# Fewer scores ahead at the start, tiles turned inside the first layers, and the last pair's lists made later, in an attention and mixture-of-experts kernel

## The chip, the cores and the metric

The kernel runs on one core of one Trainium2 chip. The metric is the device time of one execution in microseconds (us), as the median of several runs. Profiles come from one execution taken by the hardware profiler. The engines are TensorE (PE, with its weight loads shown apart as PEld), VectorE (DVE), ScalarE (ACT), GpSimd (POOL) and SyncE (SP, which here only issues transfers). Each engine works through its own instructions in the order in which the program gave them.

## What is computed

Attention with a sliding window of 128 and a linear position bias runs over 8 batches, 8 heads, 576 positions and a head size of 64. Its output, 4608 rows of 512, goes through a mixture of 8 experts: a gate picks one expert for each row, each expert is two layers with a ReLU between, and the row is scaled with the gate's probability.

```python
scores = scale * np.matmul(q, k.transpose(0, 1, 3, 2))
scores = np.where(mask, scores + bias[None], -1000000000.0)
attn = np.exp(scores - max); attn = attn / (sum + 1e-09)
x = (attn @ v).transpose(0, 2, 1, 3).reshape(4608, 512)
expert_idx = np.argmax(x @ w_gate, axis=1)
...
    h = np.maximum(x_sorted[lo:hi] @ w1[e], 0.0)
    y_sorted[lo:hi] = h @ w2[e]
return gate_w[:, None] * y
```

## The kernel before

**Order.** The program fixes the order of the instructions on each engine by the order of its own statements; nothing is rearranged afterwards. Small jobs are put into lists (`tasks` during attention, `fill` during the experts), and one entry is taken off at set points: `some()` once in each attention group, `step()` after each half product of an expert's layer.

**Attention.** Batches are taken two at a time (four pairs, `bp`), heads two at a time, which gives 16 units of four groups each, 64 groups in all. For each group `scores(i)` multiplies keys and queries into a PSUM tile `sp` (two buffers), ACT takes the exponential into `pe` (six buffers), and DVE multiplies by position factors. `values(u, half, kbs)` then multiplies with the values, and `finish(u, half)` copies the half unit out and sums the weights. The loop issues `scores(i + AHEAD)` before the values of group i, with `AHEAD = 3`. Loads for unit u + 2 are issued in unit u on SP's queue, each held back by `no_earlier_than`, a tiny transfer that waits for the product of group i + 1.

**Routing.** What `behind(bp)` lists runs during the next pair's attention: the gate, the choice of an expert, each row's place in its expert's list (`place`), and the lists themselves. `ones_at` and `ones_at2` (L1000 to L1015) make tables of ones on DVE and `enlist` (L1025) turns them into lists with matmuls. `early_table` computes the gather index of the first expert and `gather` fetches its rows from `x_rows` in DRAM with four indirect transfers on POOL. Rows reach `x_rows` by `row_out` (POOL) and `squares_out` (POOL or SP). The last pair has no attention behind which its routing could run; `with_tail` puts it into the first layer of the first expert.

**Experts.** A first group of 512 rows for each expert is `fixed[e]`; overflow of 128 rows goes to small groups between them. Both layers use seven products instead of eight for a 2 by 2 block matrix (`strassen1`, `strassen2`), each product in two halves, so 14 steps a layer, in the order of products 1, 2, 6, 5, 7, 3, 4. `prepare(g)` makes the jobs that come before: `to_scale` (DVE, L1252) and `to_columns` (PE transposes, L1265, then an ACT copy) for each of four tiles, `x_sums` (four DVE sums, of which product 6 reads the second) and `w1_sums` (eight). Products 1 and 2 read tiles 0 and 1 only. The sums of w2 and of h (L530 to L541) are needed from product 6 of the second layer. `count_all`, `check_all`, `table_further` and `pieces` compute the overflow's index. `end_of_tail` frees the routing buffers and loads the second expert's weights into that space.

Of the kernel before, what the change touches and what calls it, by code (L numbers as in the profile page):

```python
# [8 lines left out]
F32 = mybir.dt.float32  # L9
# [7 lines left out]
P = 128  # L17
# [441 lines left out]
def kernel(  # L459
# [12 lines left out]
    nc = tc.nc  # L472
# [12 lines left out]
    TPB = 2 * S // P  # L485
# [21 lines left out]
    with ExitStack() as fast:  # L507
# [504 lines left out]
        def ones_at2(bp):  # L1012
            rc, oc = slot_of[bp], oc_of[bp]
            orow = small.tile([P, TPB, P], BF16, name="gsr")
            nc.vector.tensor_tensor(  # L1015
                orow[:], K["cols"][:, None, :].to_broadcast([P, TPB, P]),
                rc[:, 0, :].unsqueeze(2).to_broadcast([P, TPB, P]), op=ALU.is_equal,
            )
            oh_of[bp] = oc, orow

        def enlist(bp):
            oc, orow = oh_of[bp]
            ps = ps_m.tile([P, 512], F32, name="m")
# [44 lines left out]
        def scales_squared(bp):  # L1068
# [10 lines left out]
            for r in range(2):  # L1079
                half = slice(r * KB, (r + 1) * KB)  # L1080
                nc.scalar.copy(sq[half].rearrange("p t k h -> p k t h"), ps5[half, :, :, r, :])  # L1081

        def squares_turned(bp, t):
            if bp in spare and t < TPB - 1:
                w = NA * PW
                flat = spare[bp].rearrange("p h n -> p (h n)")
                xs = flat[:, t * w : (t + 1) * w].rearrange("p (k w) -> p k w", k=NA)
            else:
                xs = rows.tile([P, NA, PW], F32, name="xs")
            xs_of[bp, t] = xs  # L1090
            nc.vector.transpose(
                xs[:, :, :PD].rearrange("p k (h j) -> p k h j", h=HP),
                xT[bp][:, :, t * P : (t + 1) * P].rearrange("p h (k i) -> p k h i", k=NA),
            )

        def squares_out(bp, t, eng, n=1):

            for k in range(t, t + n):
                nc.gpsimd.tensor_copy(xs_of[bp, k][:, :, PD:], sq_of[bp][:, k])  # L1099
            if n == 1:  # L1100
# [50 lines left out]

        def early_table():

# [4 lines left out]
            nc.vector.tensor_scalar_max(hole[:], hole[:], 0.0)  # L1158
            nc.vector.tensor_tensor(K["off"][:, 0:1], K["off"][:, 0:1], hole[:], op=ALU.add)
            tok = rte.tile([P, NJ], F32, name="tok_0")  # L1160
            number(tok[:], lambda k: parts[:, k, 0, :NJ])
# [92 lines left out]
        def to_columns(g, j):  # L1254
# [12 lines left out]
            else:  # L1267
                nc.vector.transpose(to.rearrange("p h (k j) -> p k h j", j=TQ), xn[:])  # L1268

        def x_sums(g):  # L1270
            x = g["xT"]
            g["xs"] = mx_pool.tile([P, 3, 2, 256], F32, name="xs")
            o = g["xs"]
            return sums_t(
                x[:, 0:2, :256], x[:, 0:2, 256:], x[:, 2:4, :256], x[:, 2:4, 256:], o[:, 0], o[:, 1], o[:, 2],
            )
# [11 lines left out]
        def prepare(g):  # L1288
# [8 lines left out]
            if n == NJ:  # L1297
                sums = later(lambda: x_sums(g), 4)
                if "ws" not in g:
                    sums += later(lambda: w1_sums(g), 8)  # L1300
                if g is fixed[1]:
                    todo[-1].append(sums.pop(0))
                    todo += [sums[k : k + 2] for k in range(0, len(sums), 2)]
                else:
                    todo += [[f] for f in sums]
            return [(g, t) for t in todo]


        def behind(bp):
# [10 lines left out]
            if bp == 0:  # L1320
                rt = [lambda t=t: squares_turned(bp, t) for t in range(TPB)]
                ro = [lambda t=t: squares_out(bp, t, nc.gpsimd) for t in range(TPB)]
                return [g3[0:1], g3[1:2], g3[2:] + t3[0:1], t3[1:], a, a2 + rt[0:1], b + rt[1:2], b2 + rt[2:3],
                        c + n + rt[3:4], [], q + p, p2 + ro[0:4], o, o2, rt[4:6], e + rt[6:8] + ro[4:8]]
            rt, ro = ([lambda t=t, f=f: f(bp, t) for t in range(TPB)] for f in (row_turned, row_out))
            if bp == 1:
                last = [lambda: squares_turned(0, TPB - 1), lambda: squares_out(0, TPB - 1, nc.gpsimd)]
                return [g3[0:1] + last, g3[1:2], g3[2:] + t3[0:1], t3[1:], a + rt[0:1], a2 + rt[1:2], b + rt[2:3],
                        b2 + rt[3:4], c + n, [], p + ro[0:2], p2 + ro[2:4] + rs[4:5], o + rs[5:6], o2 + rs[6:7], rs[7:8], e + rs[8:9]]
            return [g3, t3, a + a2, b + b2 + rt[0:1], c + n + rt[1:2], rt[2:4], p + p2 + ro[0:4], o + o2 + rs[4:6], rs[6:9],  # L1330
                    e, [early_table, lambda: gather(fixed[0], x_d[: 3 * 2 * S, :])]]

# [7 lines left out]
        NG = 4 * len(units)  # L1340
        AHEAD = 3
        for i in range(AHEAD):
            scores(i)
        route_consts()
# [4 lines left out]
        for i in range(NG):  # L1349
# [13 lines left out]
            if g == 2:  # L1363
                values(u, 0, (4,))
                finish(u, 0)
                some()
            if i + AHEAD < NG:
                scores(i + AHEAD)
            if u in (10, 11):
# [9 lines left out]
            else:  # L1379
                values(u, 1, (6, 7, 8))  # L1380
                finish(u, 1)
            if u == len(units) - 1 and g == 0:
                tasks.extend(t for _, t in prepare(fixed[0]))
            if g != 2:
# [29 lines left out]

        def strassen1(g, start=None):
            w, x, ws, xs = g["w1"], g["xT"], g["ws"], g["xs"]
            hf = F // 2
# [186 lines left out]

        self_late = []

        def with_tail(g, w2s):
# [3 lines left out]
            rt = [lambda t=t: squares_turned(bp, t) for t in range(TPB)]  # L1611
            ro = [lambda: squares_out(bp, 0, nc.sync, 4), lambda: squares_out(bp, 4, nc.sync, 4), lambda: squares_out(bp, 8, nc.sync)]
            w = [[f] for f in w2s]
            a, b, p, o = (
                [lambda f=f, f2=f2: (f(bp), f2(bp))]
                for f, f2 in ((scale_a, scale_a2), (scale_b, scale_b2), (place, place2), (ones_at, ones_at2))
            )
            c, n, q, e = ([lambda f=f: f(bp)] for f in (scale_c, count, scales_squared, enlist))
            todo = [
                [lambda k=k: gate(bp, k) for k in range(3)] + rt[0:1], [lambda k=k: turn(bp, k) for k in range(3)] + rt[1:2],  # L1620
                a, rt[2:3], b, rt[3:4], c + n, rt[4:5] + w[0], q + p + ro[0:1] + rt[8:9], rt[5:6] + o, rt[6:8] + ro[2:3],
                ro[1:2] + w[1] + w[2], e + w[3], [table_fixed] + w[4] + w[5],
            ]
            self_late.extend(w[6] + w[7])
            return [(g, t) for t in todo]
# [5 lines left out]
        for i in range(len(groups)):  # L1631
# [3 lines left out]
            if i == 0:  # L1635
                strassen1(g, start=with_tail)
                end_of_tail()
                fill.append((g, [lambda: gather(fixed[1], x_d[:, :]), self_late[0]]))
                fill.append((g, [self_late[1], count_all]))
                fill.append((g, [check_all]))  # L1640
                fill.append((g, [table_further]))
                fill.append((g, [next_groups, lambda: pieces(slice(NJ, E * NJ), "1")]))
                fill.append((g, [lambda: pieces(slice(E * NJ, NC), "2")]))
                fill.extend(prepare(fixed[1]))
                strassen2(g)
                w_of = lambda k: (w1_a, w2_a) if k % 2 == 0 else (lp["w"], lp["w"])
                load_w1(groups[2], w1_a)
# [52 lines left out]
```

## Time and profile before

| | |
|---|---|
| median of 3 runs | 686.86 us (684.91 to 687.83) |
| the profiled execution | 691.06 us, its span 689.2 us |
| mean granted TensorE clock | 0.985 |
| DMA moved | 122.00 MB, mean 177 GB/s |
| POOL gathers, L1240 | 124, 1008 ns each |
| largest single wait of PE at the start | 4.3 us, for the first queries and keys |
| PE waits in 165 to 182 us | 3.1 us, two, for DVE's scaled tiles L1252 |
| PE waits in 211 to 245 us | 2.2 and 1.4 us, for DVE |

The span goes from the first to the last instruction. PE is busy nearly always, so a job on another engine matters only where PE stands waiting for it. In the rows of the timeline the square bracket names the idle time before an instruction and what ended it. Attention lasts to about 181 us, the first expert's first layer to 211, its second to 245, and the second expert's first layer to 269 us.

### The profile page before, as it was taken

What the parts mean: (1) busy time and instruction counts of PE and PEld (TensorE: products, weight loads), DVE (VectorE), ACT (ScalarE), POOL (GpSimd) and SP (SyncE); (2) the same over time, 40 slices, a digit from 0 to 9 for tenths busy, and PEclk for the clock granted to TensorE, in tenths of its full rate; (3) what the DMA queues carried; (4) which work ended last, traced back from release to release, by engine and by line L of the source; (5) the groups of instructions that cost most, each with busy time, mean ns of one, the idle gap of its engine ahead of it and who ended that gap; (6) DMA issues with size and microseconds to landing.
All of it is one profiled execution on the core that took longest, in us unless ns stands there. A gap on an engine that the chain in (4) does not pass through costs nothing.

```text
span 689.2 us, 14460 instructions
## 1 busy us (share of the span) xinstructions
PE 655.8 (95%) x6004; PEld 548.2 (80%) x6004; DVE 379.4 (55%) x717; ACT 199.2 (29%) x365; POOL 237.6 (34%) x360
## 2 busy tenths in 40 slices
PE   5899889998999899999999999999999999999996
PEld 4778768687687788878897887888788978878893
DVE  4567769786489476614842564275148435633500
ACT  5555446465331223113202310231131123002210
POOL 8100572215001176117323702652172247023020
PEclk9999899999999999999999999999999999999999
DMA  9677987854516964185448237652844573284010
GB/s 285 200 222 192 287 241 219 289 157 149 165 22 162 386 206 140 57 292 170 155 154 301 57 129 258 212 166 63 296 137 145 178 276 97 86 305 154 1 62 8
DMA packets 63549, 122.00 MB, mean 177 GB/s; under 512 B 5905, under 2 KB 30001, under 8 KB 63474
## 3 DMA queue, kind: packets, MB, share of 16 engines
q1 hardware_dynamic: 51778, 92.78, 42.0%
q0 software_dynamic: 10544, 27.31, 12.4%
q8 instruction: 49, 0.80, 0.5%
q10 hardware_dynamic: 1152, 0.88, 0.4%
q14 instruction: 26, 0.21, 0.1%
HBM read 101.79 MB, written 19.96 MB: 177 GB/s over the span
## 4 chain that ended last, share of the span: by engine, by line
PE 75%; issue 9%; DVE 8%; DMA 4%; POOL 2%; ACT 1%; SPq 0%; POOLq 0%; DVEq 0%; ACTq 0%
PE sp L769 5%; PE at L804 5%; PE pair0b L1511 4%; PE pair0a L1511 4%; PE pair0b L1454 4%; PE pair0a L1454 4%; PE pair1a L1511 4%; PE pair1b L1511 4%; PE pair2b L1454 4%; PE pair1b L1454 4%; PE pair1a L1454 4%; PE pair2a L1454 4%; PE pair2a L1511 4%; PE pair2b L1511 4%; PE m L836 3%
## 5 line engine op out<-in xcount | busy, mean ns | idle before, releaser
L1240 POOL DMA_INDIRECT xg<-x_rows,p_idx x124 | 125.0, 1008 | 37.8 <-issue 37.5
L1534 POOL DMA_INDIRECT out_dram<-zo,s_idx x39 | 44.5, 1140 | 250.6 <-DVE zo L1525 149.6
L769 PE MATMUL sp<-q_sb,k_sb 64*64 64x192 f32 (+2 forms) x1152 | 60.2, 331 | 7.1 <-DMA q_sb<-in_qT_dram 6.9
L775 ACT ACTIVATE pe<-sp 128x768 f32<-128x768 f32 x64 | 51.9, 811 | 49.6 <-PE sp L769 46.7
L804 PE MATMUL at<-pe,v_sb 64*64 64x192 f32 (+2 forms) x1408 | 59.6, 289 | 3.4 <-issue 3.4
L778 DVE TENSOR_TENSOR pe<-pe,fac 128x768 f32<-128x768 f32 x48 | 45.5, 952 | 28.3 <-ACT pe L775 27.8
L804 PEld LDWEIGHTS at<-pe,v_sb 64*64 64x64 f32 x1408 | 48.0, 138 | 9.5 <-issue 6.9
L769 PEld LDWEIGHTS sp<-q_sb,k_sb 64*64 64x64 f32 x1152 | 42.0, 141 | 16.6 <-DMA q_sb<-in_qT_dram 4.3
L1465 ACT ACTIVATE h<-h 128x512 f32<-128x512 f32 x32 | 20.2, 631 | 41.3 <-DVE h L1464 41.3
L836 PE MATMUL m<-pe,ind 128*32 128x192 f32 (+2 forms) x704 | 29.8, 288 | 0.6 <-issue 0.6
L1252 DVE TENSOR_TENSOR xn<-xg 128x512 f32<-128x512 f32 x39 | 26.3, 676 | 3.4 <-DMA xg<-x_rows,g_idx 3.1
L836 PEld LDWEIGHTS m<-pe,ind 128*32 128x32 f32 x704 | 23.2, 110 | 3.0 <-issue 1.0
L1108 POOL DMA_DIRECT2D x_rows<-xs x40 | 21.6, 548 | 6.4 <-POOL xs L1099 1.9
L783 DVE TENSOR_TENSOR pe<-pe,fac 128x768 f32<-128x768 f32 x16 | 15.3, 955 | 15.2 <-ACT pe L775 15.1
L1268 DVE STREAM_TRANSPOSE xgT<-xn 128x512 f32<-128x512 f32 x31 | 22.1, 712 | 1.1
L538 DVE TENSOR_TENSOR w2s<-w 128x512 f32<-128x512 f32 x16 | 10.9, 684 | 19.4 <-DMA w<-in_moe_w_dram 19.4
L1099 POOL COPY xs<-sq 128x16 f32<-128x16 f32 x10 | 2.6, 258 | 53.8 <-ACT sq L1081 53.8
L1566 PE MATMUL pair2a<-w,h 128*128 128x512 f32 x48 | 21.1, 592 | 0.0
L821 ACT COPY xT<-at 128x640 f32<-128x640 f32 (+1 forms) x32 | 18.7, 585 | 6.5 <-PE at L804 4.6
L1454 PE MATMUL pair0b<-xgT,w 128*128 128x256 f32 x72 | 17.2, 382 | 0.0
L1511 PE MATMUL pair1a<-w,h 128*128 128x256 f32 x72 | 17.0, 379 | 0.0
L1454 PE MATMUL pair0a<-xgT,w 128*128 128x256 f32 x72 | 17.0, 379 | 0.0
(375 smaller groups left out, 1393.2 us busy)
## 6 DMA issues: line engine op xcount, KB each, us to landing
w<-in_moe_w_dram SPq DMA_DIRECT2D x29, 2048.0 KB, 7.9
k_sb<-in_kT_dram SPq DMA_DIRECT2D x15, 576.0 KB, 5.6
q_sb<-in_qT_dram SPq DMA_DIRECT2D x15, 576.0 KB, 5.6
v_sb<-in_v_dram SPq DMA_DIRECT2D x30, 288.0 KB, 4.5
x_rows<-xs POOLq DMA_DIRECT2D x16, 264.0 KB, 3.8
x_rows<-xs POOLq DMA_DIRECT2D x32, 66.0 KB, 4.7
x_rows<-xT SPq DMA_DIRECT2D x8, 264.0 KB, 5.2
w<-in_moe_w_dram SPq DMA_DIRECT2D x4, 512.0 KB, 7.7
```

What stands on the lines that cost most here:

```text
L769: nc.tensor.matmul(sp[c * KB : (c + 1) * KB, r, c0 : c0 + n], lhsT=k_sb[u][hs, c, kb * KB : (kb + 1) * KB], rhs=q_sb[u][hs, c, kb * KB : k ...
L775: nc.scalar.activation(pe[:], sp[:, :, :GC], AF.Exp, scale=SCALE)
L778: nc.vector.tensor_tensor(pe.rearrange("p r (k c) -> p r k c", k=2), pe.rearrange("p r (k c) -> p r k c", k=2), fac[:, h0 : h0 + 2, None, ...
L804: nc.tensor.matmul(acc[r * D : (r + 1) * D, c, lo - q0 : hi - q0], lhsT=v_sb[u][c * KB : (c + 1) * KB, kb, r * D : (r + 1) * D], rhs=pe[c ...
L836: nc.tensor.matmul(sm[32 * j : 32 * j + 32, lo - q0 : hi - q0], lhsT=none[:] if pe is None else ind[:, hp, :], rhs=fac[:, 0, :KB] if pe is ...
L1108: eng.dma_start(x_d[r0 : r0 + n * m, a * PW : (a + 1) * PW].rearrange("(k i) w -> i k w", i=TQ), xs[a * TQ : (a + 1) * TQ, p0 // TQ : p0 / ...
L1240: nc.gpsimd.indirect_dma_start(out=to, out_offset=None, in_=where, in_offset=bass.IndirectOffsetOnAxis(ap=idx, axis=0),)
L1252: nc.vector.tensor_tensor(xn[:], x, s.unsqueeze(3).to_broadcast([P, NA, HP, TQ]), op=ALU.mult)
L1268: nc.vector.transpose(to.rearrange("p h (k j) -> p k h j", j=TQ), xn[:])
L1454: nc.tensor.matmul(ps[:, f * 256 : (f + 1) * 256], lhsT=left[m][:, d, fb * P : (fb + 1) * P], rhs=right[m][:, d, :], start=(m in (1, 2, 5) ...
L1511: nc.tensor.matmul(ps[:, :256], lhsT=left[m][:, f, c * P : (c + 1) * P], rhs=right[m][:, f, :], start=(m in (1, 2, 5) and f == 0), stop=Tr ...
L1534: ins = nc.gpsimd.indirect_dma_start(out=out[:, :], out_offset=bass.IndirectOffsetOnAxis(ap=s_idx[:, g["c0"] + j : g["c0"] + j + 1], axis= ...
```

## The change

The lead of the scores is two groups in units 0 and 1 and three from unit 2 on. The loop that copies the scales into the rows becomes a function of its own, `squares_scaled`, so that all nine tiles of the last pair are given their scales at once. The first part of `early_table` becomes `early_holes`; it and the rest run one step earlier, and with them the first gather.

For the first expert, `tasks` now gets only the first three entries of `prepare(fixed[0])` (scale of tile 0; columns of 0 and scale of 1; columns of 1 and scale of 2), after group 61 instead of 60. Columns of tiles 2 and 3, the last scale and the sums of x are put into steps 0 and 1 of its first layer. `with_tail` places the rest of the last pair's routing in other steps, all of the w2 sums in the first layer, and one row write on POOL instead of SP. `ones_at`, `ones_at2` and `enlist` of the last pair go to steps 0, 1 and 5 of the second layer, and `end_of_tail` to step 5; the table and gather of the second expert follow in step 6, then the counts and further tables. Tiles 0 and 1 of the second expert are turned in steps 11 and 12, and tiles 2 and 3 in steps 0 and 1 of its own first layer, with four of its weight sums; its x sums come in steps 2 and 3.

```diff
-        AHEAD = 3
-        for i in range(AHEAD):
-            scores(i)
+        scored = [0]
+
+        def scores_to(n):
+            while scored[0] < min(n, NG):
+                scores(scored[0])
+                scored[0] += 1
+
+        scores_to(2)
...
-            if i + AHEAD < NG:
-                scores(i + AHEAD)
+            scores_to(i + (3 if u < 2 else 4))
...
-            return [g3, t3, a + a2, b + b2 + rt[0:1], c + n + rt[1:2], rt[2:4], p + p2 + ro[0:4], o + o2 + rs[4:6], rs[6:9],
-                    e, [early_table, lambda: gather(fixed[0], x_d[: 3 * 2 * S, :])]]
+            return [g3, t3, a + a2, b + b2 + rt[0:1], c + n + rt[1:2], rt[2:4], p + p2 + ro[0:4], o + o2 + rs[4:6],
+                    rs[6:9] + [early_holes], e + [early_table, lambda: gather(fixed[0], x_d[: 3 * 2 * S, :])]]
...
+        def squares_scaled(bp, t, n=1):
+
+            for k in range(t, t + n):
+                nc.gpsimd.tensor_copy(squares(bp, k)[:, :, PD:], sq_of[bp][:, k])
+
         def squares_out(bp, t, eng, n=1):
-
-            for k in range(t, t + n):
-                nc.gpsimd.tensor_copy(xs_of[bp, k][:, :, PD:], sq_of[bp][:, k])
...
-            if u == len(units) - 1 and g == 0:
-                tasks.extend(t for _, t in prepare(fixed[0]))
+            if u == len(units) - 1 and g == 1:
+                first = [t for _, t in prepare(fixed[0])]
+                tasks.extend(first[:3])
...
-            ro = [lambda: squares_out(bp, 0, nc.sync, 4), lambda: squares_out(bp, 4, nc.sync, 4), lambda: squares_out(bp, 8, nc.sync)]
+            ro = [lambda: squares_out(bp, 0, nc.sync, 4), lambda: squares_out(bp, 4, nc.sync, 4), lambda: squares_out(bp, 8, nc.gpsimd)]
...
             todo = [
-                [lambda k=k: gate(bp, k) for k in range(3)] + rt[0:1], [lambda k=k: turn(bp, k) for k in range(3)] + rt[1:2],
-                a, rt[2:3], b, rt[3:4], c + n, rt[4:5] + w[0], q + p + ro[0:1] + rt[8:9], rt[5:6] + o, rt[6:8] + ro[2:3],
-                ro[1:2] + w[1] + w[2], e + w[3], [table_fixed] + w[4] + w[5],
+                first[3] + [lambda k=k: gate(bp, k) for k in range(3)],
+                first[4] + [lambda k=k: turn(bp, k) for k in range(3)] + first[5] + first[6] + first[7] + first[8],
+                a, a2 + rt[0:1], b, b2 + rt[1:2], c + n + rt[2:3], rt[3:4] + w[0] + w[1],
+                q + p + [lambda: squares_scaled(bp, 0, TPB)], rt[4:5] + rt[8:9] + ro[0:1] + ro[2:3] + w[2],
+                rt[5:8] + ro[1:2], w[3], w[4] + w[5], w[6] + w[7],
             ]
-            self_late.extend(w[6] + w[7])
+            after_tail.extend([o[0:1], o[1:2], [], [], [], e + [end_of_tail]])
...
-                end_of_tail()
-                fill.append((g, [lambda: gather(fixed[1], x_d[:, :]), self_late[0]]))
-                fill.append((g, [self_late[1], count_all]))
-                fill.append((g, [check_all]))
-                fill.append((g, [table_further]))
-                fill.append((g, [next_groups, lambda: pieces(slice(NJ, E * NJ), "1")]))
-                fill.append((g, [lambda: pieces(slice(E * NJ, NC), "2")]))
-                fill.extend(prepare(fixed[1]))
+                todo = [t for _, t in prepare(fixed[1])]
+                sums = [f for (f,) in todo[9:]]
+                now = after_tail + [
+                    [table_fixed, lambda: gather(fixed[1], x_d[:, :])], [count_all], [check_all], [table_further],
+                    [next_groups] + todo[0], todo[1], todo[2] + [lambda: pieces(slice(NJ, E * NJ), "1")],
+                    [lambda: pieces(slice(E * NJ, NC), "2")] + sums[0:4],
+                ]
+                fill.extend((g, t) for t in now)
                 strassen2(g)
+                fill.extend((None, t) for t in [todo[3] + sums[4:], todo[4], todo[5] + todo[6], todo[7] + todo[8]])
```

## The prediction

> **What bounds the kernel now.** I read the page's busy shares and 40 slices first, then the waits of TensorE (PE) by stretch, then PE's and VectorE's (DVE's) timelines inside the stretches that lose time, and last the chain of waits.
>
> ```profile
> PE 655.8 (95%) x6004; PEld 548.2 (80%) x6004; DVE 379.4 (55%) x717; ACT 199.2 (29%) x365; POOL 237.6 (34%) x360
> ...
> PEclk9999899999999999999999999999999999999999
> ```
>
> PE is busy for 655.8 of 689.2 us, so 33 us of gaps is all that an edit of order can win at full clock. Instructions on PE stay (the added and removed ones below are moves), so the question is which gaps close and which open. The table of stretches shows where they lie:
>
> ```profile
> 13.00:30.00 17.00, 14.92 (x396) 12.97 (x399) 7.54 (x9) 9.54 (x17) 6.28 (x51) 1.00 0.76 223
> 164.00:181.00 17.00, 13.86 (x296) 11.66 (x288) 8.65 (x23) 6.30 (x13) 5.15 (x6) 0.90 0.39 97
> 181.00:211.00 30.00, 29.36 (x167) 24.09 (x166) 23.93 (x61) 8.87 (x18) 1.33 (x9) 1.00 0.35 104
> 211.00:245.00 34.00, 30.46 (x150) 26.21 (x149) 23.55 (x65) 6.55 (x14) 7.54 (x7) 0.95 0.83 274
> 245.00:269.30 24.30, 24.30 (x114) 21.11 (x113) 15.75 (x26) 8.16 (x14) 18.40 (x20) 1.00 0.44 141
> ```
>
> (columns: stretch, length, busy us of PE, weight loads, DVE, ACT, POOL, then granted clock.) The first layer of the first expert (181 to 211) and everything from 245 to the last layer run without a gap. The edit can reach gaps in three places: the first units, the entry to the first expert, and its second layer (two waits):
>
> ```profile
> 13.04 0.88 PE L769 MATMUL sp<-q_sb,k_sb 64*64 64x192 f32 x16 [1.89 <-DMA q_sb<-in_qT_dram]
> ...
> 172.72 0.66 PE L1265 MATMUL m<-ident,xn 128*128 128x128 f32 x4 [2.48 <-DVE xn L1252]
> ...
> 220.68 1.13 PE L1511 MATMUL pair1a<-w2s,hs 128*128 128x256 f32 x4 [1.35 <-DVE w2s L539]
> ...
> 226.61 1.03 PE L1142 MATMUL m<-ta,to_squares 128*128 128x7 f32 x8 [2.19 <-DVE tb L1131]
> 227.50 2.72 PE L1511 MATMUL pair0a<-w2s,hs 128*128 128x256 f32 x8
> 230.01 2.88 PE L1511 MATMUL pair0b<-w2s,hs 128*128 128x256 f32 x8
> ```
>
> The last two rows are as telling as the waits: the same eight matmuls take 1.73 us start to start elsewhere, so after the 2.19 us gap PE ran below full clock until 232.7. The stretch 164 to 181 shows it too (granted 0.90): 48 small matmuls at 175.95 took 2.22 us where 24 take 0.84.
>
> **What the Trainium skill says.** "TensorE: Matmul & The Clock Gate", Part 1, says that the array falls to half clock once an activity window of about 3.4 us has seen too little work and needs about as long to return. The trace agrees in kind: gaps of 2.48 and 2.19 us were each followed by slow matmuls, the gap of 1.35 us at 219.3 by none. The same page ("Architectural detail") says matmuls stay in program order and DVE is a strict FIFO; here PE stood 2.48 us behind one transpose with other work queued. "DMA: Bandwidth & Descriptors", section on the anatomy of a DMA from GpSimd, puts a fixed cost of about 2 us on such a write before its completion shows; the row writes here land 2.5 to 3.3 us after issue.
>
> **The change, part by part.** All sums are against the profiled execution (691.06 us, span 689.2). It is 4.2 us above the median of the three runs (686.86); I take the gain in us over to the median.
>
> *A. Scores two groups ahead in the first two units.* Before, PE does scores of group 4 (first of unit 1) before the values of group 1, and there waits 1.89 us for unit 1's queries, whose transfer was issued at 4.71 and took 8.19 us by the chain of waits. After, the values of groups 1 and 2 and the first sums (from 13.71 to 15.40 in the timeline, 1.69 us) come before those scores, so the wait is filled and 0.2 us of it is left. At group 8 two scores are issued at once and the lead is three again. Nothing is added. The price: between a group's scores and its values PE now has two other groups, 4 x 0.83 = 3.3 us. The path it must cover, from the row at 16.77: matmuls end at 17.60, exp 17.66 to 18.47, multiply to 19.47, so 1.9 us, or 2.8 with one 0.93 us factor activation ahead on ACT. Unit 2's loads are paced by a product one group later (about 2 us); they landed 6 us after issue and are read at group 8, some 10 us on. The gain lies between 0.3 (stalls of 0.2 us in a few groups) and 1.9. I take 1.5.
>
> *B. Entry to the first expert.* Before, PE's order is: values, tile 0's transposes (wait 2.48), sums, tile 1, values, sums, tiles 2 and 3 (wait 0.65), first layer at 180.66. From 170.23, when it ran dry, that is 10.43 us for 5.5 us of work (16 transposes 1.7, 56 value matmuls 2.0, two sums 1.75); the rest is waiting and slow clock. The list step and the gather are put one step earlier, but I give that nothing: the gather at 167.98 waits for the row writes of the third pair, the last issued at 164.02 and landing up to 3.3 us later, and those stay where they are; the index was ready at 166.0. So tile 0 is ready at 172.7 as before. After: values and sums 1.2 us to 171.4, wait 1.3 for tile 0, transposes 0.43, 48 value matmuls and sums 2.5, tile 1 0.43, to 176.1. Then the first layer, whose first two products need tiles 0 and 1 alone, waits 0.85 us for tile 1's copy (0.59 on ACT plus hand-overs): it was covered before and is not now. Start at 176.95, 3.7 earlier. Tiles 2 and 3 (0.87 us) move into the layer's first two steps: net 2.85. Their scales and the four sums of x (0.65 each) go to DVE there; the third product comes after 8.4 us and two more products, and by adding DVE's rows up, the sums are done 10.4 us into the layer, the product that reads them starts at 11.9. Bounds: 1.0, if the shorter waits still bring the slow clock (1.8 us), to 4.1, if the gather does start earlier. I take 2.8.
>
> *C. Second layer of the first expert.* Before, 210.95 to 244.84 is 33.9 us: 14 x 1.727 = 24.2 of products, 1.7 of transposes, 1.9 for the two index products, 0.55 for the counts; the waits of 1.35 and 2.19 and 1.8 of slow clock make up the rest. Both waits were DVE's queue: the last pair's lists (L1000 to L1015, 3.0 us from 205.64 to 208.64) stood ahead of the sums for h and w2. After, the lists come behind those. Adding DVE's rows from the layer's start T: sums of h and w2 to T+7.0, with the second sum of h, which the third product (at T+6.9) reads, at T+5.6, so the 1.35 goes; the last two w2 sums to T+8.4; lists to T+11.4. The enlisting matmuls stand on PE at T+10.4, so a new wait of 1.0 to 1.2 opens there; behind it on PE is the fourth product and all that follows. Index from the lists at T+13.1, then the four gathers on POOL (1.25 us apart); this, not the row writes, now sets them, since the last writes land near T+7.6. Weights of the second expert are issued at about T+12, as close ahead of the gathers as before (220.25 against 221.30). With the 6.9 us to landing of before, tile 0 is scaled at T+21.2 and PE asks at T+23.0: covered, with 1.8 to spare. Counts and the further table now come after, one piece to a step, and have nothing behind them that PE needs soon; the 2.19 goes. Sum: 24.2 + 0.46 (lists) + 0.55 + 0.87 (two tiles) + 1.9 + 1.2 = 29.2. In the second expert's first layer the other two tiles cost 0.87, and DVE (held by the last index product until T+29.2, then eight weight sums and a scale, 5.8 us, then two x sums) delivers the third product's operand about 0.4 late. That layer ran gapless before, so this is new. The lists leave the first layer: 0.46 back. Net 33.9 - 29.2 - 1.3 + 0.46 = 3.9; hand-overs between engines take some, so 3.6. Bounds: 1.0 (a 12 us landing) to 5.2 (no new waits).
>
> *The rest.* Splitting the scale copies from the row writes moves nine POOL copies of about 0.2 us and eight writes from SP to POOL (0.55 each, 4.4 us) in a stretch where POOL is busy 1.33 of 30 us: nothing; without that cover the gathers would start later by those 4.4. After T+55 PE has no gap to the last layer (POOL's next gathers start about 25 us before the layer that turns their tiles; it was 22 before, 246.98 against 269.3), so what is won stays won.
>
> Sum: 1.5 + 2.8 + 3.6 = 7.9, so 683.2 for the profiled execution and 679.0 for the median.
>
> **Rivals.**
> - *The new waits trip the slow clock.* Three short waits remain (1.3, 0.85 and 1.2). For: gaps of 2.2 and 2.5 did. Against: 1.35 did not. One episode costs 1.8 and DVE slips by another 1.4 behind it: 682.2.
> - *The gathers of the second expert do not do what their new place asks.* Issued within 1 us of 4 MB of weights, they may land after 12 us instead of 6.9 (4 MB at the 400 GB/s of that stretch take 10). Then tile 0 is late by 2.9, slow clock 1.8, tile 1 and the sums 1.5 more: 685.2. For: the same engines carry both. Against: the same neighbourhood gave 6.9 to 7.1 before.
> - *Slower: two ahead is too short.* If each of the eight early groups stalls PE by s, the total is 6.4 + 1.7 - 8s; it is slower than before by 0.5% once s passes 1.44, that is when scores to product takes 4.7 us. At s = 1.7: 692.4. For: in these units ACT also makes factors (0.93) and copies (0.69 and 0.43). Against: 1.9 us measured, 3.9 with all three ahead of it.
>
> **How the numbers follow.** Chances: forecast 0.68, slow clock 0.15, late gathers 0.09, slower 0.08. A measurement here tells about 0.5% (3.4 us) from no change. Faster by more: 0.97 of the first, 0.8 of the second, a seventh of the third: 0.79. Within: the rest of these, 0.12. Slower 0.09. The parts at their best (1.9, 4.1, 5.2) give 675.7, at the runs' spread 675; the upper end takes in the two middle rivals: 685.5.
>
> **What would show it.** A: the first scores of unit 1 with a wait below 0.4 us. B: the first layer starting 6.4 to 6.8 us after PE's last values of group 61, not 10.4, with one wait for tile 0 of about 1.3. C: second layer of 29 us with one wait on the list tile before the enlisting matmuls, gathers right after the index. Wrong it is if waits on products appear in the first eight groups, if granted clock stays below 1 in both stretches, or if the second expert's first layer is longer than 26 us.

## The result and the profile after

| | kernel before | changed kernel |
|---|---|---|
| median | 687.98 us (19 runs, 684.91 to 695.0) | 682.0 us (19 runs, 678.64 to 688.46) |
| ratio, 95% interval | 1 | 0.9906 (0.9882 to 0.993) |
| the profiled execution | 691.06 us, span 689.2 | 682.0 us, span 679.9 |
| its mean granted clock | 0.985 | 0.992 |

The change makes the kernel faster by 6.0 us in the medians. The two profiled executions differ by more, 9.3 us of span, because the execution profiled of the kernel before lay 3 us above its own median and that of the changed kernel on its median. This matters below. The ratios, the fit and the slope below leave out three runs of the kernel before that took more than 1.5% longer than its fastest.

The busy shares and the granted clock of the changed kernel's page:

```profile
PE 651.4 (96%) x6004; PEld 545.0 (80%) x6004; DVE 379.3 (56%) x717; ACT 199.2 (29%) x365; POOL 242.8 (36%) x368
...
PEclk9999889999999999999999999999999999999998
```

The same 6004 matmuls are busy for 4.4 us less (655.8 before). No matmul was removed, so this part of the gain points to the clock: before its last matmuls the profile of the kernel before has five stretches of 3.41 us at half clock and that of the changed kernel has two (how they are found stands with the repeats below). The other 4.9 us are idle time that closed.

The table of stretches of the changed kernel, cut at its own stage marks (the entry to the first expert, its first layer, its second layer, the second expert's first layer); columns as before, the granted clock third from the end:

```profile
161.32:174.47 13.15, 10.92 (x297) 9.57 (x292) 8.14 (x19) 6.18 (x11) 5.33 (x6) 1.00 0.46 124
174.47:204.94 30.47, 30.18 (x166) 24.94 (x167) 23.59 (x61) 10.19 (x21) 4.91 (x16) 1.00 0.37 106
204.94:233.08 28.14, 28.01 (x150) 24.40 (x149) 19.93 (x57) 5.15 (x13) 8.23 (x9) 1.00 0.85 278
233.08:259.18 26.10, 25.56 (x122) 21.82 (x122) 19.32 (x32) 8.77 (x15) 20.27 (x20) 1.00 0.58 196
```

Every stretch now has clock 1.00; before, the entry had 0.90 and the second layer 0.95. Set beside the same marks of the kernel before (us):

| stage | before | after |
|---|---|---|
| start to the entry's mark (unit 14's copy of its values on ACT) | 163.50 | 161.32 |
| entry, from there to the first product | 17.16 | 13.15 |
| first expert, first layer | 30.29 | 30.47 |
| first expert, second layer | 33.90 | 28.14 |
| second expert, first layer | 24.30 | 26.10 |
| the rest of the span | 420.0 | 420.7 |

PE's rows in the changed kernel's timeline that answer to the waits shown of before:

```profile
12.92 0.88 PE L769 MATMUL sp<-q_sb,k_sb 64*64 64x192 f32 x16
...
170.31 0.63 PE L1273 MATMUL m<-ident,xn 128*128 128x128 f32 x4 [1.56 <-DVE xn L1260]
...
174.47 1.99 PE L1472 MATMUL pair0a<-xgT,w 128*128 128x256 f32 x8 [0.67 <-ACT xgT L1274]
...
215.49 0.56 PE L1025 MATMUL m<-oc,gsr 128*128 128x96 bf16 x9
215.88 1.96 PE L1529 MATMUL pair0a<-w2s,hs 128*128 128x256 f32 x8
...
241.71 1.97 PE L1472 MATMUL pair2a<-xs,ws 128*128 128x256 f32 x8 [0.54 <-DVE xs L539]
```

The first scores of unit 1 (12.92) start without a wait, where 1.89 us stood before. The entry keeps two shorter waits, 1.56 for tile 0 and 0.67 for tile 1's copy. The second layer has lost both of its waits, and the enlisting matmuls start at 215.49, 0.19 us after the product before them could have ended (it starts at 213.57, and products are 1.73 us apart), so they hardly wait for their lists. The wait at 241.71, in the second expert's first layer, is new.

### The profile page after: what moved, and what is told of

Its sections match the earlier page's. It is cut to its first block, busy times and chain, and to the rows that moved or that the text cites. A ratio compares the mean times of both kernels' runs of the same rounds, so it can differ in the third digit from the quotient of the medians.

```text
span 679.9 us, 14461 instructions
## 1 busy us (share of the span) xinstructions
PE 651.4 (96%) x6004; PEld 545.0 (80%) x6004; DVE 379.3 (56%) x717; ACT 199.2 (29%) x365; POOL 242.8 (36%) x368
## 4 chain that ended last, share of the span: by engine, by line
PE 68%; issue 15%; DVE 6%; POOL 5%; DMA 3%; ACT 1%; ACTq 0%; POOLq 0%; DVEq 0%; SPq 0%
PE sp L769 5%; PE at L804 4%; PE pair1a L1529 4%; PE pair1b L1529 4%; PE pair0b L1472 4%; PE pair0a L1472 4%; PE pair0a L1529 4%; PE pair0b L1529 4%; PE pair2b L1472 4%; PE pair2a L1472 4%; POOL xg L1248 3%; PE pair1b L1472 3%; PE pair1a L1472 3%; PE pair2b L1529 3%; PE pair2a L1529 3%
## 5 line engine op out<-in xcount | busy, mean ns | idle before, releaser
L1114 POOL DMA_DIRECT2D x_rows<-xs x48 | 26.0, 551 | 7.4 <-DVE w L540 2.3
L1053 POOL COPY xs<-es 128x16 f32<-128x16 f32 x18 | 7.3, 407 | 28.7 <-DVE es L952 27.8
L1472 PE MATMUL pair0b<-xgT,w 128*128 128x256 f32 x72 | 17.2, 382 | 0.0
```

Of the source, the lines that this page charges most:

```text
L1114: eng.dma_start(x_d[r0 : r0 + n * m, a * PW : (a + 1) * PW].rearrange("(k i) w -> i k w", i=TQ), xs[a * TQ : (a + 1) * TQ, p0 // TQ : p0 / ...
L1472: nc.tensor.matmul(ps[:, f * 256 : (f + 1) * 256], lhsT=left[m][:, d, fb * P : (fb + 1) * P], rhs=right[m][:, d, :], start=(m in (1, 2, 5) ...
```

## The experiments

**Each part by itself.** One kernel has A alone, three leave one part out. Theory: each part gives what the sum says (1.5, 2.8, 3.6) and they add. Rival: one part carries the gain and another gives nothing, or less than nothing.

A alone is the kernel before with

```diff
-            if i + AHEAD < NG:
-                scores(i + AHEAD)
+            scores_to(i + (3 if u < 2 else 4))
```

> The kernel before with part A alone: scores two groups ahead in units 0 and 1. Theory (the forecast's sum of three independent parts): the wait for unit 1's queries falls from 1.89 us to below 0.4, every later mark of the profile comes 1.5 to 2.5 us earlier, and the time is 1.5 to 2.5 us below the kernel before (ratio 0.9965 to 0.998). Rival (the early gain is eaten by the routing of the first pair or by the transfers of units 2 and 3): the copies of units 0 to 2 come 2 us earlier and those from unit 9 on less than 1, ratio 0.999 to 1.0.

Without A is the changed kernel with the loop and `AHEAD = 3` of before.

> The changed kernel with part A undone: three groups ahead throughout. Theory: the sum of B and C stays, entry to the first expert about 3.8 us and second layer plus second expert's first layer about 4.1 us shorter than before, and the time 1.5 to 2.5 us above the changed kernel (ratio to before about 0.993 to 0.995). Rival (A is worth nothing): the same ratio as the changed kernel, 0.9906.

Without B, all four tiles and the sums stand ahead of the first layer again:

```diff
-            if u == len(units) - 1 and g == 1:
-                first = [t for _, t in prepare(fixed[0])]
-                tasks.extend(first[:3])
+            if u == len(units) - 1 and g == 0:
+                tasks.extend(t for _, t in prepare(fixed[0]))
...
-                first[3] + [lambda k=k: gate(bp, k) for k in range(3)],
-                first[4] + [lambda k=k: turn(bp, k) for k in range(3)] + first[5] + first[6] + first[7] + first[8],
+                [lambda k=k: gate(bp, k) for k in range(3)],
+                [lambda k=k: turn(bp, k) for k in range(3)],
```

> The changed kernel with part B undone: all four tiles of the first expert turned and summed before its first layer, as before; A and C stay. Theory: from the last values to the first product the 10.4 us of before return with the wait of 2.5 us for tile 0 and slow clock after it; the first layer is 0.9 us shorter than in the changed kernel; 2.8 to 3.8 us slower than the changed kernel (ratio to before about 0.995). Rival (the gather's earlier step does it, not the order of the tiles): tile 0 comes before it is asked for and at most 1 us is lost.

Without C, `with_tail` has the steps of before (the lists in the first layer), and so has the block after `strassen1`; B's tiles stay in the first two steps.

> The changed kernel with part C undone: lists of the last pair in the first layer, tables and all tiles and sums of the second expert in the second layer, as before; A and B stay. Theory: the second layer takes 33 to 34 us again with waits of over 1 us for the w2 sums and for the further table, and the time is 3.5 to 4.5 us above the changed kernel (ratio to before about 0.996). Rival (half of C's gain is only the slow clock, which is chance): the waits return without slow matmuls and 2 us are lost.

| kernel | median us (runs) | ratio to before, interval | entry | layer 1 | layer 2 | second expert, layer 1 |
|---|---|---|---|---|---|---|
| A alone | 687.0 (22) | 0.9967 (0.9943 to 0.999) | 15.58 | 30.30 | 33.89 | 24.30 |
| without A | 683.08 (19) | 0.991 (0.9883 to 0.9937) | 13.16 | 30.48 | 28.15 | 26.10 |
| without B | 681.5 (6) | 0.9879 (0.9829 to 0.9929) | 16.80 | 29.84 | 28.15 | 26.10 |
| without C | 685.46 (22) | 0.9936 (0.9913 to 0.9959) | 13.15 | 30.93 | 33.72 | 24.30 |

Each ratio is taken to runs of the kernel before made beside that kernel. The stages do what the parts say: with the repeats below taken in, the second layer is 28.1 with C and 32.2 to 33.9 without, the entry 13.2 to 13.3 with B and 15.4 to 18.5 without. In the times, single pairs are too noisy: without A (0.991) and without B (0.9879) came out level with the changed kernel (0.9906), as the rivals had it. A fit of three additive effects to the runs of before, the changed kernel, these four and the repeats below (225 runs) gives, in us saved: A 2.0 (within 0.7), B 1.3 (within 0.8), C 3.8 (within 0.8), 7.1 together. All three help; none carries the gain alone.

A alone also asked a question: its entry was 15.58, though nothing in the entry had been changed and the same waits of 2.45 and 0.65 us stood there, against 17.16 in the kernel before.

**Repeats, for the clock after a wait.** Theory: a wait of about 2.5 us at the entry is sometimes followed by slow matmuls and sometimes not, with no edit between. Rival: something that A changes decides it.

> Part B undone as in no_b, for more runs (that one had six). Theory: entry and first layer together take 46.6 us, or 48.2 with the slow clock after the 2.5 us wait, against 43.6 in the changed kernel, and the time is 2 to 4 us above it. Rival (the first reading, 681.5, stands): no slower than the changed kernel.

> The changed kernel once more, unedited, for a second profile and more runs beside the others. Theory (parts B and C are fixed lengths, the rest is chance of the clock): entry 13.15 us from the copy of unit 14's first half to the first product, first layer 30.5, second layer 28.1, second expert's first layer 26.1, each within 0.1; the marks of attention differ by a few us. Rival: these lengths vary as much as the total.

> The kernel before once more, unedited, for a second profile. Theory (fixed lengths apart from the slow clock): entry 17.2 us if the wait for tile 0 is followed by slow matmuls and 15.4 to 15.6 if not, first layer 30.3, second layer 33.9, second expert's first layer 24.3. Rival: the lengths differ by more than 0.3 us otherwise.

PE's rows in the first profile of the kernel without B:

```profile
168.21 1.11 PE L1273 MATMUL m<-ident,xn 128*128 128x128 f32 x4 [2.52 <-DVE xn L1260]
...
169.89 1.51 PE L836 MATMUL m<-pe,ind 128*32 128x192 f32 x18
```

And in the second profile of the identical kernel:

```profile
168.22 0.66 PE L1273 MATMUL m<-ident,xn 128*128 128x128 f32 x4 [2.56 <-DVE xn L1260]
...
169.22 0.83 PE L836 MATMUL m<-pe,ind 128*32 128x192 f32 x18
```

The same wait at the same place: in one execution the four transposes took 1.11 us and the 18 sums 1.51, in the other 0.66 and 0.83. That is half clock in one and full clock in the other, and 1.43 us of entry (16.80 against 15.37), with no edit between, so the rival is out.

What it goes with can be read from the granted clock in the traces. In every profile of this study its changes lie whole multiples of 3.413 us apart: the slow spells of the kernel before began at 71.57, 133.01, 173.97 and 228.58, which is 18, 12 and 16 such stretches apart, and each lasted one stretch or two. Where this rhythm lies against the kernel differs from execution to execution. Here are the two profiles of the kernel without B, cut into its stretches, counted on from a change of the clock (columns: stretch, length, busy us of PE, granted clock, DMA share and GB/s). The first:

```profile
164.77:168.18 3.41, 0.92 (x28) 1.00 0.58 150
168.18:171.59 3.41, 3.38 (x37) 0.50 0.57 167
```

And the second:

```profile
163.35:166.76 3.41, 2.31 (x70) 1.00 0.29 75
166.76:170.17 3.41, 1.95 (x38) 1.00 0.73 185
170.17:173.58 3.41, 3.33 (x80) 1.00 0.19 67
```

In the first the whole wait fell into one stretch, which left PE busy for 0.92 of 3.41 us, and the next stretch ran at half clock. In the second the same wait was split over two stretches, and no slow one followed. Over the thirteen profiles, up to 660 us, all 16 full-clock stretches with PE busy for less than 0.39 of the time were followed by one at half clock, 11 of the 27 between 0.39 and 0.585, and none of the 2402 above that. So it is the place of a wait in this rhythm, and not the wait alone, that goes with slow work; what tells the 27 in the middle apart stays open.

A repeat of the kernel before (one run, 687.64 us) had it longer still: entry 18.47 at granted clock 0.82, with two slow stretches in a row. The opposite happened in its second layer. Its rows:

```profile
224.86 1.03 PE L1142 MATMUL m<-ta,to_squares 128*128 128x7 f32 x8 [2.19 <-DVE tb L1131]
225.75 1.97 PE L1511 MATMUL pair0a<-w2s,hs 128*128 128x256 f32 x8
```

and those of the kernel without C:

```profile
218.92 1.08 PE L1148 MATMUL m<-ta,to_squares 128*128 128x7 f32 x8 [2.03 <-DVE tb L1137]
219.86 3.60 PE L1533 MATMUL pair0a<-w2s,hs 128*128 128x256 f32 x8
```

After 2.19 us of waiting the eight products ran at full speed, after 2.03 us at half. The stretches again, first the repeat of the kernel before, whose wait (222.67 to 224.86) is split over both:

```profile
220.41:223.83 3.42, 2.26 (x12) 1.00 0.99 384
223.83:227.24 3.41, 2.38 (x15) 1.00 1.02 409
```

and the kernel without C, whose wait (216.89 to 218.92) lies in the first:

```profile
216.35:219.76 3.41, 1.38 (x11) 1.00 1.02 393
219.76:223.17 3.41, 3.41 (x10) 0.50 1.01 359
```

The forecast for this repeat missed in both stages (33.9 for a layer of 32.20; 17.2 or 15.5 for an entry of 18.47), and that is the finding. Counted over the profiles: after the wait of 2.45 to 2.56 slow matmuls in 3 of 5 executions, after that of 2.03 to 2.19 in 3 of 4; after the waits of 1.34 to 1.79 that the profiles have in the same part, in none. The length alone is no safe sign, though: in the attention of the kernel before, a wait of 1.70 us that fell into one stretch was followed by half clock too:

```profile
132.20 0.66 PE L1044 MATMUL m<-ident,xT 128*128 128x128 f32 x4 [1.70 <-DVE sumT L847]
```

```profile
129.59:133.01 3.42, 1.72 (x34) 1.00 0.90 257
133.01:136.42 3.41, 3.41 (x48) 0.50 0.87 298
```

The changed kernel repeated itself within 0.2 us in every stage of the expert part (entry 13.32, then 30.48, 28.15, 26.09). Its longest wait there is 1.72 us, and the emptiest stretch there has PE busy for 0.60 of the time in one profile and 0.59 in the other. A wait of 1.56 us wholly inside one stretch would leave 0.54 at most (an estimate: 3.41 less 1.56, over 3.41), so a slow stretch is not excluded there. In these 8 runs its median was 681.85, ratio 0.9902 (0.9868 to 0.9937). The kernel without B, beside it, took 683.43 us (12 runs), ratio 0.9926 (0.9897 to 0.9954): 1.6 us more, where its first six runs had shown no loss.

**The earlier table and gather.** The prediction gave them nothing, since the gather waits for row writes. Undone by itself:

```diff
-                    rs[6:9] + [early_holes], e + [early_table, lambda: gather(fixed[0], x_d[: 3 * 2 * S, :])]]
+                    rs[6:9],
+                    e, [early_holes, early_table, lambda: gather(fixed[0], x_d[: 3 * 2 * S, :])]]
```

> The changed kernel with the first expert's table and gather put back one step later, as before; nothing else. Theory (the gather waits for the row writes, not for its index): the gather starts at the same distance from unit 14's copy, about 4.3 us, PE waits 1.6 us for tile 0, and the time is that of the changed kernel within 0.2%. Rival (the index sets it): the gather starts 1 us or more later and the wait grows by as much.

POOL's rows in this kernel:

```profile
158.42 1.09 POOL L1058 DMA_DIRECT2D x_rows<-xs  x2 [0.29 <-POOL xs L1053]
163.34 1.14 POOL L1248 DMA_INDIRECT xg<-x_rows,g_idx  x1 [3.84 <-DMA x_rows<-xs]
```

and in the changed kernel:

```profile
161.11 1.09 POOL L1058 DMA_DIRECT2D x_rows<-xs  x2 [0.29 <-POOL xs L1053]
165.61 1.45 POOL L1248 DMA_INDIRECT xg<-x_rows,g_idx  x1 [3.41 <-DVE pe L778]
```

The gather follows the last two row writes at 4.92 us in one and 4.50 in the other. In the first the row writes are named as what ended the wait; in the second a product of attention that the gather doesn't read. Where several things are awaited, the name is only that of the last one by the profile. Counted from unit 14's copy the gather came after 4.92 us here (158.42 to 163.34) and after 4.29 there (161.32 to 165.61): later with the later table, but by less than the 1 us of the rival. The entry was 13.56 against 13.15, the median 680.98 us (14 runs), ratio 0.9899 (0.9871 to 0.9927): no gain from the earlier table and gather that the times show, at most 0.4 us by the stage.

**The waits that are left.** Here the changed kernel was carried further. First, the last pair's gate matmuls were put behind the values of the last group, ahead of the first layer, and tile 0 is turned one entry later, so that PE has work while tiles 0 and 1 are scaled and copied; and two of the second expert's weight sums were put behind its x sums, since the prediction blamed the eight weight sums for the third product's wait.

```diff
-                tasks.extend(first[:3])
+                tasks.extend([first[0], [], first[1], first[2], [lambda k=k: gate(BP - 1, k) for k in range(3)]])
...
-                first[3] + [lambda k=k: gate(bp, k) for k in range(3)],
+                first[3],
...
-                fill.extend((None, t) for t in [todo[3] + sums[4:], todo[4], todo[5] + todo[6], todo[7] + todo[8]])
+                fill.extend((None, t) for t in [todo[3] + sums[4:6], todo[4], todo[5] + todo[6], todo[7] + todo[8] + sums[6:]])
```

> The changed kernel with its three remaining PE waits covered: tiles 0 and 1 of the first expert are turned after the last attention values instead of before them, the last pair's gate products stand between them and the first product, and the second expert's last two weight sums come after its x sums. Theory (a wait is worth its length where PE has other work to put into it): the waits of 1.56, 0.67 and 0.54 us go, the first layer starts with at most 0.3 us of waiting before it, and the time is 2 to 2.7 us below the changed kernel. Rival (the work put in front only moves the wait to the next step, as tile 0's and the gate's PSUM buffers are shared): the sum of PE's waits from the last values to the second product stays above 1.5 us and less than 1 us is won.

It ran in 679.25 us (6 runs), ratio 0.9862 (0.9819 to 0.9906). The entry grew to 14.32 and the first layer fell to 28.04: 1.3 us in all where 2.2 us of waits were covered, between theory and rival, since two waits came up in their place. The median is 2.6 us below that of the changed kernel beside it (681.85); with six runs, the part of this beyond 1.3 us is not shown to come from the edit. PE's rows of this kernel:

```profile
173.22 0.63 PE L1273 MATMUL m<-ident,xn 128*128 128x128 f32 x4 [0.65 <-DVE xn L1260]
...
176.22 0.43 PE L856 MATMUL m<-xT,wgd 128*32 128x128 f32 x8 [0.51 <-DVE gs L861]
```

The first is tile 1's scale on DVE, the second the gate's own PSUM buffer. And the 0.54 us before the third product stayed as it was, so the prediction's cause for it was not the true one. DVE's rows of this kernel show why:

```profile
239.22 0.69 DVE L1482 TENSOR_TENSOR h<-pair0a,s 128x512 f32<-128x512 f32 x1 [1.28 <-PE pair0a L1472]
239.83 0.68 DVE L538 TENSOR_TENSOR xs<-xgT 128x512 f32<-128x512 f32 x1
240.54 0.69 DVE L539 TENSOR_TENSOR xs<-xgT,xs 128x512 f32<-128x512 f32 x1
```

With two weight sums fewer, DVE stands idle for 1.28 us, waiting for product 2 to add it up (L1482), and the x sums queue behind that. What holds the third product back is the place of the x sums, behind product 2's result, not DVE's load. So they were moved one step up, ahead of it, and the two weight sums that stood before them went behind:

```diff
-[todo[3] + sums[4:6], todo[4], todo[5] + todo[6], todo[7] + todo[8] + sums[6:]]
+[todo[3], todo[4] + todo[5] + todo[6] + sums[4:6], todo[7] + todo[8], sums[6:]]
```

> The previous version (late_gates) with the second expert's first two x sums one step earlier, ahead of product 2's sum on DVE instead of behind it. Theory (the 0.54 us wait is that sum standing in front, not the weight sums): the wait of the third product falls below 0.2 us, the second expert's first layer takes 25.6 us instead of 26.1, and the time is 0.5 us below late_gates, 1.5 to 2.5 below the changed kernel. Rival (DVE is short of time there altogether): the wait stays at about 0.5 us.

DVE's rows of that kernel:

```profile
236.31 0.69 DVE L538 TENSOR_TENSOR xs<-xgT 128x512 f32<-128x512 f32 x1 [1.43 <-ACT xgT L1274]
237.03 0.69 DVE L539 TENSOR_TENSOR xs<-xgT,xs 128x512 f32<-128x512 f32 x1
...
238.97 0.68 DVE L1482 TENSOR_TENSOR h<-pair0a,s 128x512 f32<-128x512 f32 x1
```

The x sums now come 2 us before product 2's result, the wait is gone and the layer takes 25.31 us instead of 26.10. This kernel ran in 678.08 us (6 runs, 676.17 to 678.86), ratio 0.9841 (0.9806 to 0.9877): ahead of both kernels, and the lowest median of the study, though its interval overlaps that of the step before.

**The lists alone put back.** C moves lists and tables together. Here the lists, and with them the second expert's first table and gather, are put back as before, while the counts and further tables keep their new places:

```diff
-                now = after_tail + [
-                    [table_fixed, lambda: gather(fixed[1], x_d[:, :])], [count_all], [check_all], [table_further],
+                end_of_tail()
...
+                now = [
+                    [lambda: gather(fixed[1], x_d[:, :]), self_late[0]], [self_late[1]], [], [], [], [],
+                    [], [count_all], [check_all], [table_further],
```

> The changed kernel with the last pair's lists back in the first layer and the w2 sums behind them, as before; tables one to a step and the second expert's later tiles in its own first layer stay. Theory (two separate waits): the wait of about 1.35 us for the w2 sums returns, that of 2.2 us for the further table does not, no slow clock follows, second layer about 29.0 us and first layer 30.9, the time 1.0 to 1.8 us above the changed kernel. Rival (the lists' place is what C is worth): slow matmuls return and the second layer takes 31 us or more.

PE's rows in its second layer:

```profile
213.40 0.91 PE L1529 MATMUL pair1a<-w2s,hs 128*128 128x256 f32 x3 [1.79 <-DVE w2s L539]
...
214.37 1.89 PE L1529 MATMUL pair1b<-w2s,hs 128*128 128x256 f32 x8
216.10 1.89 PE L1529 MATMUL pair0a<-w2s,hs 128*128 128x256 f32 x8
```

The wait for the w2 sums is back (1.79; 1.35 was expected), so the layer takes 29.49 us (29.0 was expected); that for the further table is not, and the products behind run at 1.73 us start to start. So C's two waits have separate causes: the first goes with the place of the lists, the second with the place of the tables. In stages the lists are worth 1.34 us in the second layer and 0.46 in the first, 1.8 of C; the times don't separate it from the changed kernel (682.45 us in 10 runs, 0.9908, 0.9878 to 0.9938).

## Why the prediction was right

It gave 679.0 us, with 675 to 685.5; measured was 682.0. On the larger set the kernel before stands at 687.98 instead of 686.86, so the forecast gain of 7.9 us compares with one of 4.8 to 8.1 by the interval: held, at its upper edge.

*What bounds the kernel.* Right. The gain is in the stretches it named, and the rest of the span after the second expert's first layer moved by 0.7 us only.

*A, 1.5.* Right in its mechanism: the first scores of unit 1 wait for nothing (below 0.4 was asked), and no product in the first eight groups waits for its exponential, so the slower case (two ahead too short) did not occur. The entry's mark is a poor place to read its worth, since one to three slow stretches lie before it in each profile: 160.3 us on average with A (ten profiles), 161.8 without (three). Group 23's exponential comes before any slow stretch in all but one of the thirteen. Its row in the kernel before and in the changed kernel:

```profile
57.76 0.81 ACT L775 ACTIVATE pe<-sp 128x768 f32<-128x768 f32 x1 [0.33 <-PE sp L769]
...
55.59 0.81 ACT L775 ACTIVATE pe<-sp 128x768 f32<-128x768 f32 x1 [0.33 <-PE sp L769]
```

On average it starts at 54.5 us with A (52.7 to 55.8) and at 56.6 without (55.4 to 57.8), a gain of 2.1. The fit of the times has 2.0 (within 0.7), so 1.5 was a little low.

*B, 2.8.* Right in its steps: waits of 1.56 and 0.67 where 1.3 and 0.85 were forecast; the first product at 174.47, some 6.9 us after the last values of group 61 (the first 32 of 40 value matmuls that start at 166.36, so done by about 167.6; 6.4 to 6.8 was the sign to look for, and the wait for tile 0 was 0.26 longer than forecast); the earlier gather worth next to nothing. The tiles moved into the layer cost 0.64 us there (30.48 against 29.84) instead of 0.87. What was mis-sized is how much of it an average execution can win: "the rest is waiting and slow clock" took the slow clock of one execution as part of the wait. Between executions at full clock B is worth 15.5 - 13.2 - 0.64 = 1.7 us, against the worst seen 18.47 - 13.2 - 0.64 = 4.6. The times, which mix them, say 1.3 (within 0.8): half of the forecast.

*C, 3.6.* Right as a whole: 33.9 - 28.14 + 0.46 - 1.80 = 4.4 us by the stages of a pair with slow clock, 2.7 with the repeat whose layer took 32.20, and 3.8 (within 0.8) in the times. Two terms were off and partly cancel, by luck, as do B's and A's errors in the sum. The new wait for the lists was put at 1.0 to 1.2 us and was 0.19. DVE's rows of the changed kernel:

```profile
204.82 0.68 DVE L530 TENSOR_TENSOR hs<-h 128x512 f32<-128x512 f32 x1
...
214.08 1.35 DVE L1015 TENSOR_TENSOR gsr<-cols_b,rc 128x1152 bf16<-128x1152 bf16 x1
...
217.02 0.17 DVE L1136 CAST g_idx<-ta 128x4 int32<-128x4 f32 x1
```

DVE began its sums with the layer (T = 204.94) and had the lists done at T + 10.5, not T + 11.4; the index followed at T + 12.1 instead of 13.1 and the gathers at T + 12.5. The other term is the second expert's first layer: 26.10 us, past the 26 that the prediction named as a sign against it. The forecast had 24.3 + 0.87 + 0.4 = 25.6. It did not turn the result, but the reason given, "eight weight sums and a scale", was wrong: the experiments with the sums put it on the order of two entries in DVE's queue.

*The rivals.* No wait of the changed kernel tripped the slow clock: 1.00 in all four stretches, in both of its profiles. The gathers of the second expert landed 7.0 us after issue (median; 6.9 forecast) and the scaling of tile 0 began at T + 21.3 and was done at T + 21.9. The margin was thin, though: with the list wait gone PE came to tile 0's transposes at T + 21.8, not 23.0, and they started 0.26 us later than the product before them allowed (227.02, after 225.03 and 1.73), where 1.8 us to spare were forecast. The weights were issued at T + 7.3, not 12, so the two were less close than that rival assumed.

*From the profile to the median.* This is the weakest step: "I take the gain in us over to the median". The profiled execution of before had slow clock in both stretches and lay 3 us above its median, so a sum made against it includes gains that an average execution can't make. The profiles differ by 9.3 us, the medians by 6.0. The Trainium skill, "TensorE: Matmul & The Clock Gate", Part 1, has two states, half and full clock, set by an activity window of about 3.4 us that runs freely, without regard to the kernel. The halved rates after some waits agree with the two states (1.51 us against 0.83 for the same 18 sums). The rule of its section on oscillation, no idle gaps of PE above about 3.4 us, would have let all these waits pass, and the measurement decides against it: 2.03 us was enough in the kernel without C, 1.70 in the attention of the kernel before. A window that runs freely is what the traces show: the clock changes in steps of 3.413 us whose place against the kernel differs between executions, and slow work follows where a wait empties enough of one step.

## What to carry to other kernels

Once the busiest engine is at 95%, look for the waits it has by stretch, and for each ask which single instruction stands in the wrong place of the queue that feeds it; moving two x sums ahead of one result took a whole wait away, where moving two weight sums out of the way took nothing. Before taking a profile's gain over to the median, ask whether its stretches had full clock, and price waits that can leave PE idle for more than some 1.4 of 3.41 us (0.415 of the stretch, the border seen here) as the wait plus a chance of slow work behind it. A repeat of an unedited kernel is the cheapest experiment there is when a stage moves that no edit touched.

## What the runs showed of the hardware that was not expected

A wait of the same length at the same instruction was followed by half clock in some executions and not in others (3 of 5 after about 2.5 us, 3 of 4 after 2.0 to 2.2). The clock is granted in stretches of 3.413 us on a rhythm of its own; a stretch at half clock followed when PE had been busy for less than 0.39 of the stretch before (16 of 16), sometimes between 0.39 and 0.585 (11 of 27), and never above (none of 2402). The busy time of PE is modelled, so the border is not sharp. The cost was 1.4 us for one slow stretch (16.80 against 15.37) and 3.0 for two (18.47 against 15.5); the most that one can cost is half of 3.41 us, an estimate from its length and clock.

The spread of the times, a standard deviation of 2.1 to 2.6 us in the kernels with ten runs or more, goes with the granted clock: 0.001 of mean granted clock goes with 0.60 us, close to the 0.68 us that 0.001 of 682 us is, so lost clock is lost time nearly in full. The changed kernel's mean clock is 0.9914 (27 runs), that of before 0.9871 (98 runs); at equal clock it is 4.0 us faster (within 0.7), so about 2.6 of the mean difference of 6.6 us comes with the higher clock. In the profiles the slow stretches of the entry and the second layer are the ones that went, since no stretch there is empty enough any more in the changed kernel's two profiles; that this makes up all of the 2.6 us is not shown.
